# Blank records by scatter at steps 25 to 28 in place of eight clears at the start (chunk attention, then a cosine router)

## The chip, the cores and the metric

The kernel runs on one core of a Trainium2 chip. The metric is the device time of one execution in microseconds; the kernel before took 654.62 us in the median of three runs (653.24 to 658.43).

## The reference

Attention in chunks of 64, over 8 batches, 8 heads, 576 positions and 64 values per head; its output, 4608 tokens of 512 values, goes to a router that gives each token to one of 8 experts, a two-layer network with weights of its own.

```python
scores = scale * np.matmul(q_c, k_c.transpose(0, 1, 2, 4, 3))     # chunks of 64
attn = np.exp(scores - max); attn = attn / (sum + 1e-09)
x = (attn @ v_c)  ->  (4608, 512)

xn = x / (np.linalg.norm(x, axis=-1, keepdims=True) + 1e-06)
en = expert_emb / (np.linalg.norm(expert_emb, axis=-1, keepdims=True) + 1e-06)
logits = xn @ en.T / tau
expert_idx = np.argmax(logits, axis=1)
gate_w = softmax(logits)[np.arange(N), expert_idx]
for e in range(E):                      # E = 8, D = 512, F = 1024
    mask = expert_idx == e
    h = np.maximum(x[mask] @ w1[e], 0.0)
    out[mask] = gate_w[mask, None] * (h @ w2[e])
```

## The kernel before

All data are float32. The work has two stages.

**The attention stage** goes over 36 tiles of 128 tokens (NT = 36) in a software pipeline: a loop over steps t from -3 to 38, in which each step does a part of several tiles. For tile t + 7 it issues the loads of k and q (`load_qk`, L591; on the POOL queue from tile 4 on), for tile t + 5 those of v (`load_v`, L606; on the SP queue up to step 25, on POOL's from step 26). PE transposes k and q of tile t + 3 (L617), computes the scores of tile t + 2 (L633), transposes the weights of tile t (L659) and multiplies them with v (L672, `values`). DVE writes the result to `xr`, a ring of 8 slots of one tile each (L683), and POOL writes each token's number beside it (the iota at L689). PE transposes x of the tile before for the router (L701).

After every four tiles the router works on them as a batch: logits (L716), the choice of the expert (`pick`, L745 to L749), and two steps later `place`, which counts how many tokens of each expert came before and so gives each token its row (`dest`, L786). The counts are matmuls into `rt_ps`, a PSUM tile that the logits also use. From step 6 on `put` (L821) then sends one tile a step to DRAM: an indirect DMA on the POOL queue that writes each of the 128 records to its own row of `spots`. A record is 576 floats (2304 B): x, the logits, the square sum and the token's number. `spots` has R = 4864 rows for each expert, and behind them 64 spare rows from row SPARE on. A row number of SPARE or above is dropped by the scatter's bound. At step t it is tile t - 6 that is put, and step t + 2 reuses its slot in `xr`, so the scatter must have landed by then.

**The expert stage** works on blocks of two groups of 64 tokens, each group of one expert: it reads the rows of `spots` (`load_rows`, L153 and L159, on SP), computes the hidden layer and the result (L253, L342, L413), and scatters the rows to the output by token number (L432). The first four blocks (NE = 4) are fixed in advance as the first four groups of experts 0 and 7: rows 0 to 255 of each. Their loads are issued while the attention still runs: `load_early` at steps 26, 27, 28 and 33. They count on those rows being complete at step 25. For that, `count_early` at step 25 (L805 to L811) looks at how many tokens each expert has by then (the 20 tiles placed); where an expert has fewer than 256, it raises its count, so that later tokens go behind row 255. A place in the first 256 rows where no token came must hold a blank record: zeros, with a token number out of range.

Ahead of all that, `clear_first` writes such blank records to the first 256 rows of both experts and to the spare rows: nine DMAs of 64 records on the SP queue, two at each step from step 1 on. At the end of the attention stage `pad_places` does the same for the last, incomplete group of each expert, by four indirect DMAs with row numbers `pad_h`, most of which fall out of range.

The order of the instructions is the program's order on every engine; the queues of SP and POOL are worked through in order, and a DMA that must wait holds what stands behind it. On SP the first weights (w1 at step 28, w2 at step 30, 2 MB for each of two experts) stand behind the early loads. In `put`, a scatter is declared free of the early loads issued before it; an early load waits for all the scatters put before it.

Of the kernel before, what the change touches and what calls it, by code (L numbers as in the profile page):

```python
# [9 lines left out]
FP32 = mybir.dt.float32  # L10
BF16 = mybir.dt.bfloat16
I32 = mybir.dt.int32
AF = mybir.ActivationFunctionType
ALU = mybir.AluOpType
# [4 lines left out]
P = 128  # L19
# [6 lines left out]
def kernel(  # L26
# [11 lines left out]
    nc = tc.nc  # L38
    B, H, S, Dh = q.shape
    E, D = moe_expert_emb.shape  # L40
# [7 lines left out]
    G = P // 2  # L48
# [5 lines left out]
    NE = 4  # L54
# [23 lines left out]
    R = N + G * NE  # L78
    SPARE = E * R
# [38 lines left out]
    second = keep.tile([P, 1], FP32, name="second")  # L118
# [5 lines left out]
    def load_first(buf, rows):  # L124

        for s in range(2):
            e = (0, E - 1)[s]
            nc.sync.dma_start(out=whole(buf[s]), in_=rows[:, e : e + 1, :], max_dma_last_dim=4096)
# [41 lines left out]
    def first_rows(s, j, n):  # L170
        r0 = (0, E - 1)[s] * R + G * j
        return spots[r0 : r0 + G * n, :]
# [277 lines left out]
    with (  # L450
# [15 lines left out]
        blank = one.tile([P, W], FP32, name="blank")  # L466
# [18 lines left out]
        io = one.tile([P, NST], FP32, name="io")  # L485
# [10 lines left out]
        e_0 = one.tile([P, 1], FP32, name="e_0")  # L496
# [11 lines left out]
        full = one.tile([P, E], FP32, name="full")  # L508
# [2 lines left out]
        base_h = one.tile([P, E // 2], FP32, name="base_h")  # L511
        in_g = one.tile([P, 1], FP32, name="in_g")
        e_p = one.tile([P, 1], FP32, name="e_p")

        def constant_parts():
            nc.gpsimd.iota(io_i, pattern=[[1, NST]], base=0, channel_multiplier=0)
            nc.gpsimd.iota(part_i, pattern=[[0, 1]], base=0, channel_multiplier=1)
            nc.gpsimd.memset(blank, 0.0)
            nc.gpsimd.memset(blank[:, D + TOK : D + TOK + 1].bitcast(I32), NO_ROW)
            yield  # L520
            make_upper_triangular(nc, sltb, val=1.0, diag=False)
            nc.gpsimd.memset(onesb, 1.0)
            nc.gpsimd.tensor_copy(io, io_i)
            nc.gpsimd.tensor_copy(at, part_i)
            yield
            nc.gpsimd.tensor_scalar(pref, io[:, 0:E], -1.0, float(E), ALU.mult, ALU.add)
            nc.gpsimd.tensor_scalar(e_base, io[:, 0:E], float(R), None, ALU.mult)
            nc.gpsimd.memset(before, 0.0)
            nc.gpsimd.memset(eqb_all[:, 0], 0.0)
            nc.gpsimd.memset(ones, 1.0)  # L530
            yield
            nc.gpsimd.memset(jump[:, 1], 1.0)
            nc.gpsimd.memset(nb[:, 0:1], float((SPARE + R) // G))
            yield
            nc.gpsimd.tensor_scalar(second, at, float(G), None, ALU.is_ge)
            nc.gpsimd.tensor_scalar(is_0, at, 2.0, None, ALU.is_lt)
            yield
            nc.gpsimd.tensor_scalar(lim, at, -float(P), float(G * NE), ALU.mult, ALU.add)
            nc.gpsimd.tensor_scalar(step, second, -2.0, 1.0, ALU.mult, ALU.add)
            yield  # L540
            nc.gpsimd.tensor_scalar(first_s, second, -1.0, 1.0, ALU.mult, ALU.add)
            nc.gpsimd.tensor_scalar(back, io, -1.0, float(NST - 1), ALU.mult, ALU.add)
            yield
            nc.gpsimd.tensor_scalar(more_g, back, float(LEAST - NE), None, ALU.is_ge)
            nc.gpsimd.tensor_scalar(pair_g, back, float(LEAST - NE), None, ALU.is_equal)
            yield
            nc.gpsimd.tensor_tensor(more_g, more_g, pair_g, ALU.add)
            nc.gpsimd.tensor_tensor(pair_g, back, more_g, ALU.subtract)
            yield
            nc.gpsimd.memset(more_e[:, NSW - 1 : NSW], 1)  # L550
            nc.gpsimd.tensor_scalar(e_0, second, float(E - 1), None, ALU.mult)
            yield
            nc.gpsimd.tensor_scalar(e_1, e_0, 1.0, None, ALU.add)
            nc.gpsimd.tensor_scalar(ends_e, io[:, 0:E], 0.0, None, ALU.is_equal)
            yield
            nc.gpsimd.tensor_scalar(full, io[:, 0:E], float(E - 1), None, ALU.is_equal)
            nc.gpsimd.tensor_tensor(ends_e, ends_e, full, ALU.add)
            yield
            nc.gpsimd.tensor_scalar(done, ends_e, float(NE), None, ALU.mult)
            nc.gpsimd.tensor_scalar(ends_e, ends_e, is_0, None, ALU.mult)  # L560
            yield
            nc.gpsimd.tensor_scalar(in_g, second, -float(G), at, ALU.mult, ALU.add)
            nc.gpsimd.tensor_scalar(e_p, second, float(R), None, ALU.mult)
            yield
            nc.gpsimd.tensor_scalar(
                base_h, io[:, 0 : E // 2], 2.0 * R, e_p, ALU.mult, ALU.add
            )

        def clear_first():

            for j in range(NE):
                for s in range(2):
                    nc.sync.dma_start(out=first_rows(s, j, 1), in_=blank[0:G])
                    yield
            nc.sync.dma_start(out=spots[SPARE : SPARE + G, :], in_=blank[0:G])

        before = one.tile([P, E], BF16, name="before")
        qk_t, qkT, st = {}, {}, {}
# [221 lines left out]
        to_put = []  # L800

        def count_early():

            cnt = rt_ps[:, 3, 0]
            nc.tensor.matmul(cnt, lhsT=onesb, rhs=before, start=True, stop=True)  # L805

            nc.vector.tensor_scalar(full, cnt, -1.0, lim, ALU.mult, ALU.add)
            nc.vector.tensor_scalar(full, full, 0.0, float(P), ALU.max, ALU.min)
            with nc.allow_low_precision("whole numbers up to 36 + 128"):
                nc.vector.tensor_tensor(eqb_all[:, 0], full, ends_e, ALU.mult)  # L810
                nc.vector.tensor_tensor(before, before, eqb_all[:, 0], ALU.add)  # L811
# [6 lines left out]
        def put(n):  # L818

            for at, m in to_put[:n]:  # L820
                ins = nc.gpsimd.indirect_dma_start(  # L821
                    out=spots,
                    out_offset=bass.IndirectOffsetOnAxis(ap=at, axis=0),
                    in_=m,
                    in_offset=None,
                    bounds_check=SPARE - 1,
                    oob_is_err=False,
                )
                tc.declare_no_dep(ins.ins, group="spots", reason="each token has its own place")
                tc.add_to_no_dep_group("spots", ins.ins)  # L830
                for e in early_ins:
                    tc.declare_no_dep(
                        ins.ins, e.ins, reason="no place of these groups"
                    )
            del to_put[:n]
# [207 lines left out]
        early_t = 26  # L1043
# [6 lines left out]
        for t in range(-3, NT + 3):  # L1050

            if 0 <= t < NT:
                turn_a(t)
            if t == early_t - 1:
                count_early()

            for w in ahead_v[t]:
                load_v(w, nc.sync if t < early_t else nc.gpsimd)
            if t + 3 < NT:
                turn_qk(t + 3)  # L1060
                if t + 7 < NT:
                    load_qk(t + 7)
            if t - 2 in ends:
                logits(ends[t - 2])
            if t == NT:
                turn_x(t - 1)
            early_parts(t, 0)
            if 0 <= t + 2 < NT:
                scores(t + 2)
            if t - 2 in ends:  # L1070
                copy_logits(ends[t - 2])
            if 0 <= t - 1 < NT - 1:
                turn_x(t - 1)
            if t - 3 in ends:
                place(ends[t - 3])
            if 0 <= t < NT:
                values(t)
            if t == NT - 8:
                load_first(w1_sb, w1_rows)
            if t == NT - 6:  # L1080
                load_first([w[0] for w in w2_sb], w2_rows)
            if 0 <= t + 2 < NT:
                weights(t + 2)
            if t - 2 in ends:
                pick(ends[t - 2])
            if early_t <= t < early_t + XBUF:
                load_early(t - early_t)

            put(1 if t < NT - 2 else 2)
            if t == NT - 3:  # L1090
                turn_xb(0)
                load_early(XBUF)
            if t == NT - 1:
                turn_xb(1)
            early_parts(t, 1)
            if t == -2:
                turn_experts()
            if t >= 0:
                next(constants, None)
            if t >= 1:  # L1100
                next(clears, None)
                next(clears, None)
# [151 lines left out]
```

## Time and profile before

| What | Value |
|---|---|
| median of three runs | 654.62 us (653.24 to 658.43) |
| the profiled execution | 659.4 us, its span 657.6 us |
| PE busy | 620.0 us, 94% of the span |
| DVE, ACT, POOL busy | 427.6, 430.4, 183.8 us |
| attention stage | to about 180 us |
| DMA | 112.68 MB, 171 GB/s in the mean |
| clears of `spots` on SP | 20.4 to 33.6 us |
| step 25 to step 28, on PE | about 114 to 133 us |

The span is what the profile's times count from; the profiled execution's own time is a little longer than it. A line of a timeline gives the start in us, the duration in us, the engine, the line of the kernel, the operation with output and input, and the count; in brackets stands the idle time of the engine before it and what ended it. "SPq" is the SP queue, whose instructions issue DMAs. A line by stretches gives, for each engine, the busy time and the number of instructions.

### The profile page before, as it was taken

The page shows a single profiled execution, that of the slowest core. Times are in us where ns is not written, and L with a number is a line of the kernel's source. Part 1 is how long each engine was busy: PE and PEld are TensorE (multiplying, and loading weights), DVE is VectorE, ACT ScalarE, POOL GpSimd, SP SyncE. Part 2 cuts the span into 40 slices and gives each one's busy share as a digit, 9 for nine tenths or more (in the row PEclk, how much of TensorE's full clock was granted, in tenths as well). Part 3 has the DMA queues.
Part 4 walks back from the last instruction along what each step waited for, and adds up shares of the span by engine and source line. Part 5 has one row for each costly group of instructions (what it writes and reads, how often), then busy time and mean ns, then how long its engine had stood idle before and what let it go on. Part 6 is the DMA issues. An engine that isn't in the chain of part 4 may idle for free. (4 is left out here: it accounts for less than half of the span.)

```text
span 657.6 us, 24868 instructions
## 1 busy us (share of the span) xinstructions
PE 620.0 (94%) x9744; PEld 351.0 (53%) x9744; DVE 427.6 (65%) x1140; ACT 430.4 (65%) x758; POOL 183.8 (28%) x262
## 2 busy tenths in 40 slices
PE   6999998988799999999999999999999999999994
PEld 5777777865444445545555666444444444444441
DVE  4887888876479645656795466979645667565430
ACT  5766766755124767677767776777777677767650
POOL 7668887843221001002020102213001021000101
PEclk9999999989999999999999999999999999999998
DMA  9999898898518711111878111785921115411101
GB/s 252 321 276 268 260 280 265 260 340 323 214 38 303 299 44 55 39 46 38 304 262 321 59 41 45 288 308 197 350 78 59 42 44 176 165 42 35 50 27 42
DMA packets 91696, 112.68 MB, mean 171 GB/s; under 512 B 49260, under 2 KB 69484, under 8 KB 91560
## 3 DMA queue, kind: packets, MB, share of 16 engines
q1 hardware_dynamic: 79512, 71.99, 33.7%
q0 software_dynamic: 12016, 38.89, 17.2%
q8 instruction: 81, 1.33, 0.8%
q14 instruction: 55, 0.45, 0.2%
q10 hardware_dynamic: 32, 0.02, 0.0%
HBM read 334.71 MB, written 22.69 MB: 543 GB/s over the span
## 5 line engine op out<-in xcount | busy, mean ns | idle before, releaser
L413 PE MATMUL y_ps<-w,hT 128*32 128x512 f32 (+1 forms) x2368 | 280.6, 586 | 0.6 <-DMA w<-in_moe_w_dram 0.2
L361 ACT ACTIVATE h<-C 64x256 f32<-64x256 f32 x264 | 179.1, 679 | 72.8 <-DVE C L374 70.0
L413 PEld LDWEIGHTS y_ps<-w,hT 128*32 128x32 f32 x2368 | 94.9, 110 | 151.9 <-issue 132.9
L432 POOL DMA_INDIRECT out_dram<-y,spot x36 | 37.4, 1039 | 389.8 <-ACT y L425 314.3
L342 PE MATMUL h<-w,S 128*32 128x256 f32 x1056 | 106.5, 379 | 0.8 <-DVE w L291 0.8
L342 PE MATMUL h<-sums,xbT 128*32 128x256 f32 x1056 | 106.4, 379 | 0.6 <-DVEq L299 0.6
L374 DVE TENSOR_TENSOR C<-C,h 128x256 f32<-128x256 f32 x231 | 96.0, 416 | 11.6 <-PE h L342 4.4
L368 DVE STREAM_TRANSPOSE hT<-h 128x512 f32<-128x512 f32 x66 | 46.7, 708 | 54.8 <-ACT h L361 54.0
L342 PE MATMUL h<-w,xbT 128*32 128x256 f32 x1056 | 82.0, 379 | 0.0
L342 PEld LDWEIGHTS h<-w,S 128*32 128x32 f32 x1056 | 50.2, 110 | 22.6 <-DVE w L291 1.3
L342 PEld LDWEIGHTS h<-sums,xbT 128*32 128x32 f32 x1056 | 49.8, 110 | 22.7 <-DVEq L299 1.9
L342 PEld LDWEIGHTS h<-w,xbT 128*32 128x32 f32 x1056 | 44.4, 110 | 30.7 <-issue 8.4
L227 DVE TENSOR_SCALAR rn<-rn 128x1 f32<-128x1 f32 x37 | 5.6, 150 | 81.1 <-ACT rn L224 81.1
L425 ACT ACTIVATE y<-y_ps,gate 128x512 f32<-128x512 f32 x36 | 24.8, 688 | 43.7 <-issue 36.2
L342 PE MATMUL h<-sums,S 128*32 128x256 f32 x528 | 53.1, 379 | 0.0
L203 DVE STREAM_TRANSPOSE xbT<-xin 128x256 f32<-128x256 f32 x73 | 46.5, 675 | 0.5 <-DVE hT L368 0.5
L821 POOL DMA_INDIRECT spots<-xr,dest x36 | 37.4, 1039 | 29.0 <-DVE dest L786 9.9
L224 ACT ACT_TABLE_LOAD x34 | 43.6, 1283 | 0.9 <-issue 0.4
L231 ACT ACT_TABLE_LOAD x34 | 43.6, 1283 | 0.6
L703 ACT COPY xT<-tr 128x512 f32<-128x512 f32 x36 | 21.1, 586 | 33.7 <-PE tr L701 27.6
L591 POOL DMA_DIRECT2D kx<-in_k_dram x36 | 32.0, 890 | 12.2 <-PE tr L617 10.9
L591 POOL DMA_DIRECT2D qx<-in_q_dram x40 | 34.3, 861 | 0.7 <-PE tr L617 0.6
(204 smaller groups left out, 808.3 us busy)
## 6 DMA issues: line engine op xcount, KB each, us to landing
w<-in_moe_w_dram SPq DMA_DIRECT2D x74, 2048.0 KB
next_w<-in_moe_w_dram SPq DMA_DIRECT2D x67, 2048.0 KB
xin<-spots SPq DMA_DIRECT2D x158, 64.0 KB
qx<-in_q_dram POOLq DMA_DIRECT2D x32, 256.0 KB
v<-in_v_dram SPq DMA_DIRECT2D x58, 128.0 KB
kx<-in_k_dram POOLq DMA_DIRECT2D x28, 256.0 KB
spots<-blank SPq DMA_DIRECT2D x9, 144.0 KB
spot<-spots SPq DMA_DIRECT2D x80, 4.0 KB
```

The source lines that it names most:

```text
L203: nc.vector.transpose(xT[:, :, cols].rearrange("p c (b i) -> p b c i", i=Q), t[:, s * (D // 2) : (s + 1) * (D // 2)].rearrange("p (b i c) ...
L224: nc.scalar.activation(rn, spot[:, j % SPOTS, SQ : SQ + 1], AF.Sqrt)
L231: nc.scalar.activation(sh, sh, AF.Exp, accum_out=gate)
L342: nc.tensor.matmul(ps[t0 : t0 + Q], lhsT=a[:, c, s], rhs=w[:, r], start=c == 0, stop=c == KD // 2 - 1,)
L361: nc.scalar.activation(h[b][G * v : G * v + G, s].rearrange("p (k i) -> p k i", i=Q), x[G * s : G * s + G].rearrange("p (i k) -> p k i", i=Q),
L368: nc.vector.transpose(hT.rearrange("p k (s b i) -> p b s k i", b=2, i=Q)[:, b], h[b].rearrange("p s (k i) -> p s k i", i=Q),)
L374: nc.vector.tensor_tensor(out, a, b, op)
L413: nc.tensor.matmul(ps[Q * r : Q * r + Q, 0:w], lhsT=d["hT"][:, c, Q * t0 : Q * t0 + Q], rhs=w2_sb[s][buf_of(j)][:, c, d0 : d0 + w], start= ...
L425: nc.scalar.activation(y[:, 0:w], ps[:, 0:w], AF.Copy, scale=gate_of.pop(j))
L432: ins = nc.gpsimd.indirect_dma_start(out=to, out_offset=bass.IndirectOffsetOnAxis(ap=at, axis=0), in_=y[:, 0:w], in_offset=None, bounds_ch ...
L591: eng.dma_start(out=x[done : done + n], in_=src[b, :, s : s + n, :].rearrange("h p d -> p h d"),)
L821: ins = nc.gpsimd.indirect_dma_start(out=spots, out_offset=bass.IndirectOffsetOnAxis(ap=at, axis=0), in_=m, in_offset=None, bounds_check=S ...
```

## The change

The eight clears of the first rows go; the clear of the spare rows stays. In their place `count_early` works out, for every place of the first four groups, whether a token has come: `place_f` is the place's number in its expert's rows, `cnt_f` the expert's count, and `row_f` the row in `spots`; where the place is under the count, SPARE is added, so that the row is dropped. That gives 128 row numbers for each of the four groups of the pair of experts (`pad_f`), and at steps 25 to 28, after the tile's own scatter, one scatter of `blank` is put by them. Three operations for the constants are added on POOL at steps 15 and 16.

```diff
+        e_r = one.tile([P, 1], FP32, name="e_r")
+        cnt_f = one.tile([P, 1], FP32, name="cnt_f")
+        place_f = one.tile([P, NE], FP32, name="place_f")
+        row_f = one.tile([P, NE], FP32, name="row_f")
+        pad_f = one.tile([P, NE], I32, name="pad_f")
...
+            yield
+
+            nc.gpsimd.tensor_scalar(place_f, io[:, 0:NE], float(G), in_g, ALU.mult, ALU.add)
+            nc.gpsimd.tensor_scalar(e_r, e_0, float(R), None, ALU.mult)
+            yield
+            nc.gpsimd.tensor_scalar(row_f, place_f, e_r, None, ALU.add)
 
         def clear_first():
 
-            for j in range(NE):
-                for s in range(2):
-                    nc.sync.dma_start(out=first_rows(s, j, 1), in_=blank[0:G])
-                    yield
             nc.sync.dma_start(out=spots[SPARE : SPARE + G, :], in_=blank[0:G])
+            yield
...
             nc.tensor.matmul(cnt, lhsT=onesb, rhs=before, start=True, stop=True)
 
+
+            nc.vector.tensor_copy(full, cnt)
+            nc.vector.tensor_tensor(cnt_f, full[:, E - 1 : E], full[:, 0:1], ALU.subtract)
+            nc.vector.scalar_tensor_tensor(
+                out=cnt_f, in0=cnt_f, scalar=second, in1=full[:, 0:1], op0=ALU.mult, op1=ALU.add
+            )
+            nc.vector.tensor_scalar(place_f, place_f, cnt_f, float(SPARE), ALU.is_lt, ALU.mult)
+            nc.vector.tensor_tensor(pad_f, place_f, row_f, ALU.add)
             nc.vector.tensor_scalar(full, cnt, -1.0, lim, ALU.mult, ALU.add)
...
             put(1 if t < NT - 2 else 2)
+            if early_t - 1 <= t < early_t - 1 + NE:
+                j = t - (early_t - 1)
+                to_put.insert(0, (pad_f[:, j : j + 1], blank))
+                put(1)
```

## The prediction

> **What bounds the kernel now.** I read the page first (engine shares, slices), then busy time by stretch, the stages in which the edit lies, and there the timelines of PE, POOL, SP and DVE with the idle before each instruction.
>
> The page and the stretches (columns: stretch, its length, busy us and count of PE, PEld, DVE, ACT, POOL, granted clock, DMA share, GB/s):
>
> ```profile
> PE 620.0 (94%) x9744; PEld 351.0 (53%) x9744; DVE 427.6 (65%) x1140; ACT 430.4 (65%) x758; POOL 183.8 (28%) x262
> ...
> 20.00:40.00 20.00, 18.59 (x447) 15.94 (x450) 15.44 (x36) 13.60 (x32) 12.14 (x33) 1.00 1.08 317
> 60.00:80.00 20.00, 18.75 (x444) 15.64 (x446) 16.77 (x42) 14.02 (x31) 17.64 (x32) 1.00 0.88 257
> 140.00:160.00 20.00, 15.31 (x323) 11.77 (x318) 13.35 (x36) 10.27 (x24) 6.01 (x11) 0.91 0.91 347
> 240.00:260.00 20.00, 20.00 (x260) 8.91 (x254) 9.51 (x27) 13.94 (x23) 1.03 (x2) 1.00 0.14 39
> ```
>
> PE is the bound: 20.0 of 20 us in the expert stage (from about 180 us) and 18.6 to 18.8 in the attention stage. So a gain or loss counts only as PE idle time before 180 us; later nothing catches it up. The hole in PE is 140 to 160 us, after the four steps that get the new scatters.
>
> Where the clears stand, the PE timeline at the values (L672) of tiles 4, 8, 12, 16:
>
> ```profile
> 30.57 1.05 PE L672 MATMUL pv<-v,aT 64*64 64x65 f32 x32
> 47.05 0.70 PE L672 MATMUL pv<-v,aT 64*64 64x65 f32 x32
> 63.44 1.10 PE L672 MATMUL pv<-v,aT 64*64 64x65 f32 x32
> 79.89 0.70 PE L672 MATMUL pv<-v,aT 64*64 64x65 f32 x32
> ```
>
> Four tiles take 16.48, 16.39 and 16.45 us. The first four follow directly on the clears, whose issues end at 33.6 us, with the DMA share at 1.08 of 1; the others run long after. They differ by 0.1 us: the full DMA doesn't reach PE.
>
> The stretch of the new scatters, POOL's timeline, then SP's:
>
> ```profile
> 118.76 1.05 POOL L821 DMA_INDIRECT spots<-xr,dest  x1 [0.37 <-DMA v<-in_v_dram]
> 124.19 1.05 POOL L821 DMA_INDIRECT spots<-xr,dest  x1 [0.94 <-DVE rs L681]
> 128.85 1.05 POOL L821 DMA_INDIRECT spots<-xr,dest  x1 [0.18 <-POOL xr L689]
> 133.52 1.05 POOL L821 DMA_INDIRECT spots<-xr,dest  x1 [0.18 <-POOL xr L689]
> 135.75 1.05 POOL L821 DMA_INDIRECT spots<-xr,dest  x1 [0.35 <-POOL xr L689]
> 141.96 0.13 POOL L689 IOTA xr<- 128x1 int32 x1 [5.15 <-DMA spots<-xr,dest]
> 184.14 0.98 POOL L821 DMA_INDIRECT spots<-blank,pad_h  x1 [0.30 <-issue]
> ```
>
> ```profile
> 123.17 1.27 SPq L153 DMA_DIRECT2D xin<-spots  x2
> 128.35 1.12 SPq L153 DMA_DIRECT2D xin<-spots  x2
> 132.89 1.13 SPq L128 DMA_DIRECT2D w<-in_moe_w_dram  x2
> 134.86 8.35 SPq L153 DMA_DIRECT2D xin<-spots  x2
> ```
>
> The scatters of steps 25 to 29 (tiles 19 to 23) stand on a POOL with almost no slack: 0.37, 0.94, 0.18, 0.18, 0.35 us. At steps 26 to 28 POOL also issues the v loads (1.5 us a step), so a step costs it 4.66 us (124.19 to 128.85, 128.85 to 133.52).
>
> DVE and PE:
>
> ```profile
> 115.14 0.22 DVE L807 TENSOR_SCALAR full<-rt_ps,lim 128x8 f32<-128x8 f32 x1
> 141.99 0.69 DVE L683 TENSOR_TENSOR xr<-pv,rs 128x512 f32<-128x512 f32 x1 [1.60 <-DMA spots<-xr,dest]
> ```
>
> ```profile
> 115.41 1.08 PE L716 MATMUL rt_ps<-xT,enT 128*32 128x128 f32 x32 [0.64 <-DVE full L807]
> 142.82 0.63 PE L701 MATMUL tr<-ident,xr 128*128 128x128 f32 x4 [2.67 <-DVE xr L683]
> ```
>
> This decides: `xr` has 8 slots, so tile 30 can be written only when tile 22's scatter (133.52) has landed. It lands at about 141.9, 8.4 us after its start, because 4 MB of w1 were put in flight at 132.89. DVE waits 1.60 us for it and PE 2.67. A later scatter of tile 22 moves PE directly.
>
> **What the Trainium skill says.** "DMA: Bandwidth & Descriptors", section "Queues, rings and completion order": each DMA engine goes round between the queue rows with work, a packet at a time, and takes a ring's descriptors in order. The trace agrees in kind: a scatter lands in 4.4 us (118.76 to SP's wake at 123.17) without the weight load and in 8.4 us beside it. The same page, "Anatomy of one DMA — SWDGE (gpsimd) path", puts about 2.0 us fixed on such a DMA; here the last blank scatter, mostly dropped rows, starts at 184.14 and SP, which waits for it, goes on at 186.78: 2.6 us. "VectorE: DVE Perf Modes", section on the TRN2 errata, says that a small operation pays a fixed latency per instruction; here dependent ones of 128x8 start 0.20 to 0.28 us apart.
>
> **The change part by part.**
> *Removed:* eight clears of 64 x 2304 B, 1.18 MB, at 20.4 to 31.5 us on SP: eight issues of about 0.6 us, 4.9 us of a queue that otherwise waits for PE to free v slots. At 317 GB/s the bytes are 3.7 us of DMA. By the 16.48 against 16.39 us above I take 0.1 us gained; bounds 0 and 3.7.
> *POOL constants:* three operations of about 0.25 us at steps 15 and 16, where POOL still has waits: 0.
> *DVE at step 25:* five operations ahead of L807, four depending each on the one before. At 0.22 us, 1.1 us. PE's logits matmul (L716) already waits 0.64 us for L807 (they share `rt_ps`), so that wait grows by 1.1; PE has no other idle there. Bounds 0.3 and 1.3. It is part of the slip below, not added to it.
> *Four scatters:* 0.98 us by the pad_h row, 1.05 by the neighbours, and a gap of 0.2 to 0.3: 1.25 us each, on POOL behind the token's scatter of the step. From the reference's inputs the 20 tiles counted give experts 0 and 7 384 and 320 tokens, over the 256 cleared places, so all 512 rows fall out of range and no byte is written; only the instruction and its completion cost. That a dropped row is cheap in a DMA I take from the 2.6 us.
>
> POOL's schedule, in the times of before: scatter 19 at 118.76, pad to 121.05. Tile 20's waits for `dest` and DVE, 1.1 later: 125.3 (POOL is ready at 124.7). Then 4.66 + 1.25 a step: tile 21's 131.2, tile 22's 137.1, and tile 23's at 137.1 + 2.23 + 1.25 = 140.6. Slips: 1.1, 2.4, 3.6, 4.9.
>
> SP: the early loads of rows wait for all scatters put before, blank ones too. The first goes from 123.17 to about 123.8, the second from 128.35 to about 130 (blank at 126.4, behind the token's rows until 129.5); w1 stands behind it on SP, so 132.89 becomes about 134.5. Behind w1: the third rows, w2 and the fourth rows. w1 is used at 156.7 and w2 at 180.6; before, w2 waited for w1 and went at 152.8, so w1 has some 4 us to spare. Nothing there is late.
>
> Tile 22's scatter at 137.1 now starts 2.6 us after w1 instead of 0.6. With 8.4 us it lands at 145.5, a slip of 3.6; tile 23's, which before started 2.9 us after w1, took 9.6 (135.75 to 145.4), so 9 is as fair: 146.1, a slip of 4.2. Tile 23's lands at about 140.6 + 9.3 = 149.9 against 145.4: 4.5. From there the chain feeds itself: tile 24's scatter follows tile 30's iota, and tile 32 waits for it (before by 0.21 us on DVE). I see no slack up to the last `dest` that takes it back. Slip on PE 4.5 us, less 0.1: +4.4. Bounds: +1.1 (scatter delay absorbed, DVE alone) and +8 (w1 holds tile 22's rows longer, and PE's clock falls further after the longer stall; PE's transposes took 1.06 instead of 0.60 us just after 142.8).
>
> Sum against the profiled execution: 659.4 us (span 657.6 and 1.8 around it) + 4.4 = 663.8. It ran 4.8 us above the median of the runs; the difference is carried to the median: 654.6 + 4.4 = 659.0.
>
> **Rivals.** A measurement tells about 1% (6.5 us) from no change.
> 1. *POOL's slip, as worked out:* 659.0, its own range 656.5 to 662.5. Chance 0.48.
> 2. *Absorbed.* Because SP starts w1 later, tile 22's rows might get ahead of most of its packets and land in 4 to 5 us (137.1 + 5 = 142.1, as before). Then only DVE's 1.1 us is left, partly in the stall: 655.5. For it: 4.4 us without weights. Against it: the scatter is later than w1's issue. Chance 0.22.
> 3. *Other side: the clears held the first loads.* DMA at 1.08 in 20 to 40 us; kx and qx of tiles 5 to 8 queue beside 1.18 MB. Up to 3.7 us come back if those loads land after PE wants them, and it outweighs the loss only if the scatter slip also is under 2 us: 654.6 - 3.7 + 1.1 = 652.0. Against it: the equal four-tile times, and a single 1.17 us wait for v, at 20.55, for loads issued before the clears. Chance 0.15.
> 4. *A new chain of waits:* w1 outlasts tiles 22 to 25, each pair of scatters adds 2 to 3 us more, and the clock sags: 4.4 + 5 = 664. Chance 0.15.
>
> **The numbers.** The likeliest gives 659.0. The range runs from rival 3's 652.0 to a little over rival 4, 665.0. Over 661.2: a fifth of case 1 and most of case 4, 0.23. Under 648.1: a piece of case 3, 0.04. Within: 0.73.
>
> **What would show it.** Right: tiles 4 to 16 at 16.4 us per four; PE's wait for `full` at 1.5 to 1.8 us instead of 0.64; tile 22's scatter 3 to 4 us later; w1's issue 1 to 2 us later; the stall before tile 30 some 3 us longer; the same PE time from 190 us to the end. Wrong: an unmoved IOTA wait end at 142 (rival 2), four-tile times under 16 us before 64 us (rival 3), or stalls that grow again at tiles 32 to 34 (rival 4). A blank scatter taking much more than 1 us on POOL, or 4 us to land, breaks the price that all this rests on.

## The result and the profile after

The changed kernel takes 661.41 us in the median (659.09 to 663.74, 17 runs), the kernel before in the same runs 657.61 (652.17 to 661.67, 17 runs). The ratio is 1.0059, with a 95% interval of 1.004 to 1.0078: some 3.9 us slower, 0.6%. The forecast was +4.4 us, with a chance of 0.73 that the change stays within 1%; the median of 654.6 from which it started was that of three runs.

The pair of profiles doesn't show this. The profiled execution after took 659.09 us, the fastest of its 17 runs, and its span is 657.3 us against 657.6. So the profiles have to be read stage by stage. First the page's shares and the stretches after, with the same columns as before:

```profile
PE 618.9 (94%) x9744; PEld 344.2 (52%) x9744; DVE 426.6 (65%) x1145; ACT 428.9 (65%) x758; POOL 189.2 (29%) x269
...
20.00:40.00 20.00, 19.78 (x475) 16.93 (x475) 16.40 (x37) 14.61 (x34) 13.10 (x34) 1.00 0.98 271
60.00:80.00 20.00, 19.20 (x491) 16.40 (x493) 17.23 (x42) 14.91 (x34) 17.77 (x31) 1.00 1.00 275
140.00:160.00 20.00, 16.49 (x346) 12.78 (x349) 13.18 (x34) 10.27 (x23) 6.44 (x11) 0.83 0.93 351
```

PE is busier in 20 to 40 us (19.78 against 18.59), where the clears are gone, but also in 60 to 80 us, far from them. The clock in 140 to 160 us is lower, 0.83 against 0.91. PE's timeline at the values of tiles 4, 8, 12 and 16:

```profile
30.39 1.05 PE L680 MATMUL pv<-v,aT 64*64 64x65 f32 x32
46.06 0.69 PE L680 MATMUL pv<-v,aT 64*64 64x65 f32 x32
61.35 0.69 PE L680 MATMUL pv<-v,aT 64*64 64x65 f32 x32
76.60 0.69 PE L680 MATMUL pv<-v,aT 64*64 64x65 f32 x32
```

Four tiles take 15.67, 15.29 and 15.25 us, not the 16.4 that was forecast. The kernel reaches the count of step 25 3.7 us sooner than before. How much of that belongs to the change is what the experiments have to tell.

The stretch of the new scatters, POOL's and SP's timelines after:

```profile
114.40 1.05 POOL L837 DMA_INDIRECT spots<-xr,dest  x1 [0.18 <-POOL xr L697]
115.75 1.01 POOL L837 DMA_INDIRECT spots<-blank,pad_f  x1 [0.30 <-DMA v<-in_v_dram]
120.54 1.05 POOL L837 DMA_INDIRECT spots<-xr,dest  x1 [0.26 <-POOL xr L697]
126.60 1.05 POOL L837 DMA_INDIRECT spots<-xr,dest  x1 [0.18 <-POOL xr L697]
132.68 1.05 POOL L837 DMA_INDIRECT spots<-xr,dest  x1 [0.18 <-POOL xr L697]
136.06 1.02 POOL L837 DMA_INDIRECT spots<-xr,dest  x1 [0.17 <-POOL xr L697]
141.38 0.13 POOL L697 IOTA xr<- 128x1 int32 x1 [4.30 <-DMA spots<-xr,dest]
```

```profile
127.59 1.14 SPq L153 DMA_DIRECT2D xin<-spots  x2
131.15 1.13 SPq L128 DMA_DIRECT2D w<-in_moe_w_dram  x2
```

And the operations of DVE and PE that wait:

```profile
111.41 0.22 DVE L823 TENSOR_SCALAR full<-rt_ps,lim 128x8 f32<-128x8 f32 x1
141.41 0.69 DVE L691 TENSOR_TENSOR xr<-pv,rs 128x512 f32<-128x512 f32 x1 [5.21 <-DMA spots<-xr,dest]
```

```profile
111.69 1.08 PE L724 MATMUL rt_ps<-xT,enT 128*32 128x128 f32 x32 [1.10 <-DVE full L823]
142.25 1.09 PE L709 MATMUL tr<-ident,xr 128*128 128x128 f32 x4 [6.31 <-DVE xr L691]
```

A blank scatter takes 1.01 us and a gap of 0.30 on POOL. Four of them that wrote all their rows would add 1.18 MB to the queue that takes POOL's transfers. Its line of the page, first before, then after, has the same 38.89 MB, so the rows are dropped:

```profile
q0 software_dynamic: 12016, 38.89, 17.2%
```

```profile
q0 software_dynamic: 12336, 38.89, 17.5%
```

POOL's steps are 6.06 and 6.08 us long (120.54, 126.60, 132.68) where they were 4.66, and DVE waits 5.21 us for tile 22's scatter where it waited 1.60. Counted from the count's operation (L823 at 111.41, before L807 at 115.14), the scatters of tiles 20 to 23 come at 9.1, 15.2, 21.3 and 24.7 us against 9.1, 13.7, 18.4 and 20.6, and w1 at 19.7 against 17.8. Tile 30 is written at 30.0 against 26.9: 3.1 us later. The five new operations that stand ahead of the count's come on top: 1.05 us from their first start, at 110.36, to L823.

One more thing appears that the profile of before did not show. PE stands in the result of the fifth block:

```profile
236.13 9.18 PE L413 MATMUL y_ps<-w,hT 128*32 128x512 f32 x62 [3.96 <-DMA w<-in_moe_w_dram]
```

Before, it was:

```profile
238.92 6.63 PE L413 MATMUL y_ps<-w,hT 128*32 128x512 f32 x58 [0.24 <-DMA w<-in_moe_w_dram]
```

From the fourth block's output to the fifth's it is 19.6 us after and 14.0 before; an undisturbed block takes 12.9.

### The profile page after: what moved, and what is told of

Same layout as the page of the kernel before. It is cut to its first block, busy times and chain, and to the rows that moved or that the text cites. A ratio compares the mean times of both kernels' runs of the same rounds, so it can differ in the third digit from the quotient of the medians.

```text
span 657.3 us, 24875 instructions
## 1 busy us (share of the span) xinstructions
PE 618.9 (94%) x9744; PEld 344.2 (52%) x9744; DVE 426.6 (65%) x1145; ACT 428.9 (65%) x758; POOL 189.2 (29%) x269
## 3 DMA queue, kind: packets, MB, share of 16 engines
q0 software_dynamic: 12336, 38.89, 17.5%
## 5 line engine op out<-in xcount | busy, mean ns | idle before, releaser
L413 PEld LDWEIGHTS y_ps<-w,hT 128*32 128x32 f32 x2368 | 90.6, 110 | 157.9 <-issue 136.4
L342 PEld LDWEIGHTS h<-w,S 128*32 128x32 f32 x1056 | 48.7, 110 | 24.3 <-DVE w L291 1.5
L342 PEld LDWEIGHTS h<-w,xbT 128*32 128x32 f32 x1056 | 43.0, 110 | 32.3 <-issue 9.0
L203 DVE STREAM_TRANSPOSE xbT<-xin 128x256 f32<-128x256 f32 x73 | 44.2, 643 | 0.5 <-DVE hT L368 0.5
L709 PE MATMUL tr<-ident,xr 128*128 128x128 f32 x144 | 23.3, 286 | 12.5 <-DVE xr L691 10.5
```

The source lines that it names most:

```text
L203: nc.vector.transpose(xT[:, :, cols].rearrange("p c (b i) -> p b c i", i=Q), t[:, s * (D // 2) : (s + 1) * (D // 2)].rearrange("p (b i c) ...
L342: nc.tensor.matmul(ps[t0 : t0 + Q], lhsT=a[:, c, s], rhs=w[:, r], start=c == 0, stop=c == KD // 2 - 1,)
L413: nc.tensor.matmul(ps[Q * r : Q * r + Q, 0:w], lhsT=d["hT"][:, c, Q * t0 : Q * t0 + Q], rhs=w2_sb[s][buf_of(j)][:, c, d0 : d0 + w], start= ...
```

## The experiments

They ran in three sets of four, each set beside the kernel before on one chip. The medians of before were 657.09, 663.85 and 656.70 us, so kernels are compared by their ratios, and closely only within a set. The runs are called e1 to e12, in the order in which they stand here. "Measured" is the ratio to before, with its 95% interval.

**First set: the parts (e1 to e4).** e1 is the kernel with the clears gone and nothing in their place; of the change only the three constants on POOL stay. Against the changed kernel:

```diff
-            nc.vector.tensor_copy(full, cnt)
...
-            nc.vector.tensor_tensor(pad_f, place_f, row_f, ALU.add)
...
-                to_put.insert(0, (pad_f[:, j : j + 1], blank))
-                put(1)
```

> Leaves out the blank records of the first groups altogether (no clears, no row numbers, no blank scatters); with these inputs every one of those rows gets a token. Theory (POOL's slip is the loss, the clears are hidden): ratio 0.998 to 1.001, PE's time at tile 25's step within 1 us of before's typical. Rival (the clears hold the first loads): ratio 0.994 or less, and four tiles in about 15.3 to 15.7 us between tiles 4 and 16, as in the one profile of the changed kernel, where before's has 16.4. If so, the changed kernel's scatters cost more than the 0.6% that is seen.

Measured: 0.9963 (0.9941 to 0.9984), 655.16 us. The clears did cost, about 0.37% or 2.4 us (1.1 to 3.9), though less than the 0.6% at which the rival began. The 16.4 us did not hold as a mark: with the clears, tiles 8 to 12 took 15.45 and 15.56 us in the profiles of the next two kernels.

e2 has the clears and the scatters together (the change, with the eight clears put back):

```diff
         def clear_first():
 
+            for j in range(NE):
+                for s in range(2):
+                    nc.sync.dma_start(out=first_rows(s, j, 1), in_=blank[0:G])
+                    yield
```

> Both: the eight clears stay and the four blank scatters with their row numbers are added. Theory: the loss is all from what is added, ratio 1.005 to 1.008, tile 22's scatter lands some 4 us later relative to step 25, PE waits 5 to 6 us before tile 30. Rival (clears cost something too): 1.008 to 1.013, clearly above the changed kernel.

Measured: 1.0085 (1.0058 to 1.0113), 662.92 us: what is added costs 5.6 us (3.8 to 7.4). Tile 30 is written 30.0 us after the count's operation, as in the changed kernel.

e3 has the row numbers alone, with the clears and without the scatters (the same, with `to_put.insert` and its `put` left out):

> Clears stay; the five DVE operations at step 25 and the three constants on POOL are added, no blank scatter. Theory: PE's wait for the count at step 25 grows by 1.1 us, most of it taken up in the stall before tile 30: ratio 1.000 to 1.002. Rival (the DVE operations are the loss): 1.004 or more.

Measured: 1.0028 (1.0007 to 1.0048), between the two expectations. About 1.8 us of the loss (0.5 to 3.2) are the numbers', the three constants on POOL with them. That leaves 0.57%, 3.7 us, for the scatters. DVE's wait in this kernel's timeline is the short one again:

```profile
138.42 0.69 DVE L695 TENSOR_TENSOR xr<-pv,rs 128x512 f32<-128x512 f32 x1 [2.14 <-DMA spots<-xr,dest]
```

That is 26.5 us after its count's operation (111.88): the 3.5 us up to 30.0 come with the scatters.

e4 is the changed kernel again:

> The changed kernel once more, for a second profile and to be compared with its parts in the same runs. Theory: ratio 1.004 to 1.008; the stall before tile 30 on DVE is 4 to 6 us again, while the time at which step 25 is reached differs from the first profile by some us, since it differs from run to run. Rival (the early lead of 4.8 us at step 25 in the first profile belongs to the change): step 25's count at 110 to 111 us again, against 115 for kernels with clears.

Measured: 1.0047 (1.0027 to 1.0067). The parts add up: -0.37 + 0.85 = +0.48%. The count's operation came at 113.3 us, not at 111.4; with the clears it came at 111.9 (e3), 113.8 (e2) and 115.1 (before). So most of the 3.7 us of lead in the first pair of profiles was chance. DVE waits 5.53 us before tile 30, again 30.0 us after the count.

**Second set: POOL's queue, SP's order, the clears doubled (e5 to e8).** In e5 the v loads of steps 26 to 28 go from POOL to SP:

```diff
-                load_v(w, nc.sync if t < early_t else nc.gpsimd)
+                load_v(w, nc.sync if t < early_t + 3 else nc.gpsimd)
```

> The changed kernel with the v loads of steps 26 to 28 issued on SP, ahead of each step's early load, instead of POOL. That takes 4.6 us of issues off POOL in the very steps of the blank scatters and leaves their number and order as they are. Theory (the loss is POOL's queue running late): tile 22's scatter starts before or with w1, the wait of DVE before tile 30 falls from 5.2 to 5.5 us to under 2, and the ratio to before falls from 1.005 to 0.997 to 1.001. Rival (the blank scatters cost as DMAs, by holding the early loads on SP): the wait before tile 30 stays above 4 us, ratio 1.003 to 1.007.

Measured: 0.9987 (0.9959 to 1.0015): no loss is seen against before, though the same blank scatters are put in the same places. DVE has no wait before tile 30:

```profile
144.13 0.69 DVE L691 TENSOR_TENSOR xr<-pv,rs 128x512 f32<-128x512 f32 x1
```

POOL's steps are 4.57 us now, and tile 22's scatter starts at 134.35, 0.9 us before w1 (135.23) instead of 1.5 us after it. A smaller wait, 0.97 us, is found at tile 32. The edit moves two things, POOL's queue and SP's: tile 22's scatter starts 19.8 us after the count (21.3 in the changed kernel), and w1 20.6 us after it (19.7).

In the next run but one, e7, the attention stage is that of the changed kernel, on the same chip, and there DVE waits:

```profile
147.00 0.69 DVE L691 TENSOR_TENSOR xr<-pv,rs 128x512 f32<-128x512 f32 x1 [5.01 <-DMA spots<-xr,dest]
```

That is 33.7 us after its count's operation; e5 has 29.5. Beside the changed kernel's profiles from outside this set (30.0 to 30.5 us) e5 gains little, and there is one profile of each, so the comparison is good only within the set.

e6, the kernel before with the same move:

> The kernel before with the same move of the v loads. Theory: the stall of 1.6 to 2.1 us on DVE before tile 30 goes too, as tile 22's scatter starts some 4 us sooner, ahead of w1: ratio 0.993 to 0.998. Rival (w1's traffic decides, not POOL's queue): 0.999 to 1.002, the wait merely found at another tile.

Measured: 0.9982 (0.9961 to 1.0003), at the line between the two. The stall before tile 30 is gone here too, but a wait of 0.96 us stands two tiles later, and the end hardly moves. Something else had to hold the end.

e7, another order on SP in the expert stage:

> The changed kernel, with one order on SP altered in the expert stage: the second layer's weights of block 4 are asked for ahead of the rows of block 8. In every profile but that of before, PE stands 4 us in block 4's result for an issue that SP reaches some 51 to 53 us after the last blank scatter of the attention stage. Theory now: the end is set by SP's chain of loads from that last scatter on, so whatever delays the attention's tail is carried by SP and not by PE; with the order altered PE's stall of 4 us and the slower clock after it go, ratio to before 0.992 to 0.998. Rival (PE's own lateness carries the loss, as the prediction had it): the stall is waiting that PE would do anyway, ratio 1.003 to 1.007 as for the changed kernel.

```diff
-                    if n + XBUF < NJ:
+                    if n + XBUF < NJ and j != NE - 1:
                         load_x(n + XBUF)
...
                 load_w2(next_of(j))
+            if j == NE - 1:
+                load_x(n + XBUF)
```

Measured: 1.0046 (1.0019 to 1.0074). Taken alone this speaks for the rival, but the changed kernel did not run in this set, in which before was 7 us slower than in the others, and the profile had the block's stall gone. The third set has both kernels.

e8, each clear of the kernel before done twice:

> The kernel before with each of the eight clears followed by another of the same size to rows of experts 3 and 4 that are written over later: the removed cost doubled. Theory from the first runs (the clears cost 0.2 to 0.6% by filling the DMA just as PE wants its next instructions and rows): ratio 1.003 to 1.008, and PE's gap in the middle of tile 5's values (0.5 to 2.2 us with the clears, 0 or 1.4 without) at 1 us or more. Rival (no such cost; the difference without the clears is chance): 0.999 to 1.001.

```diff
                     nc.sync.dma_start(out=first_rows(s, j, 1), in_=blank[0:G])
+                    r0 = (3, 4)[s] * R + G * j
+                    nc.sync.dma_start(out=spots[r0 : r0 + G, :], in_=blank[0:G])
                     yield
```

Measured: 1.0073 (1.0039 to 1.0106), so clears do cost. But the gap in tile 5's values was not there. The timelines of POOL and of DVE show another way:

```profile
46.78 1.11 POOL L823 DMA_INDIRECT spots<-xr,dest  x1 [7.60 <-DMA v<-in_v_dram]
...
50.61 0.69 DVE L685 TENSOR_TENSOR xr<-pv,rs 128x512 f32<-128x512 f32 x1 [4.41 <-DMA spots<-xr,dest]
56.26 0.69 DVE L685 TENSOR_TENSOR xr<-pv,rs 128x512 f32<-128x512 f32 x1 [2.56 <-DMA spots<-xr,dest]
```

The first scatter stands 7.6 us on POOL for a DMA, 2.7 to 5 us later than the 41.8 to 44.1 us in the profiles of before, of the changed kernel and of the first set. The issues of the doubled clears run up to 41 us here, and the scatter must follow all of them; the trace names a v load, so that this was the wait is likely and not shown. `xr`'s ring runs full behind it. With eight clears this wait isn't seen: the first scatter waits 1.4 to 1.8 us in all five profiles with them, for ACT or DVE. So doubling shows that clears cost, and not how eight do.

**Third set: the end of the chain (e9 to e12).** e9 is the changed kernel once more:

> The changed kernel as it is, so that the next three can be read beside it on one chip. Expected ratio 1.004 to 1.008, as in both sets of runs so far.

Measured: 1.0087 (1.0055 to 1.0118).

e10 has e7's order:

> The changed kernel with block 4's second weights asked for ahead of block 8's rows, again, now beside the changed kernel: the first run gave 1.0046 on another chip, where the changed kernel itself was not run, and its profile showed the 4 us stall in block 4's result gone. Theory (SP's chain carries the end): 0.3% or more under the changed kernel in the same runs. Rival (no effect; PE carries it): within 0.2% of it.

Measured: 0.9962 (0.9942 to 0.9982), 1.2% under the changed kernel in the same set, and under before. On SP the request for w2 now follows the weights of the first layer at once. First the changed kernel's line, then e10's:

```profile
236.02 1.76 SPq L177 DMA_DIRECT2D w<-in_moe_w_dram  x2
```

```profile
230.62 1.34 SPq L177 DMA_DIRECT2D w<-in_moe_w_dram  x2
```

In the changed kernel PE goes on at 236.13, 0.1 us after SP reaches the request, and from 236 to 240 us the DMA moves 4 GB/s. So PE waits for SP to come to this load, which carries a condition (`cond` in `load_when`), and not for weights to arrive. The outputs of the fourth and fifth block, in POOL's timeline, first of the changed kernel:

```profile
227.18 0.98 POOL L432 DMA_INDIRECT out_dram<-y,spot  x1 [11.08 <-DMA xin<-spots]
246.80 0.98 POOL L432 DMA_INDIRECT out_dram<-y,spot  x1 [18.64 <-ACT y L425]
```

and of this kernel:

```profile
227.65 0.98 POOL L432 DMA_INDIRECT out_dram<-y,spot  x1 [11.07 <-DMA xin<-spots]
240.56 0.98 POOL L432 DMA_INDIRECT out_dram<-y,spot  x1 [11.93 <-ACT y L425]
```

19.6 us become 12.9, from nothing but an order on SP, though both attention stages end within half a microsecond of each other (last blank scatter at 181.88 and 182.36). PE had been early and waited for SP. In the ten profiles without this order (the changed kernel's and before's among them), PE's wait for w2 ends 54.3 to 55.6 us after the start of the attention stage's last blank scatter (before: 184.14 to 238.92; after: 181.88 to 236.13). In between SP issues the row loads and the weights in order. (The 51 to 53 us in the expectation of e7 count from SP's first load behind that scatter.)

How long PE waits there differs: 2.2 to 4.6 us in six of the ten, but only 0.20 to 0.24 in before's profile and in e5, e6 and e8, which are all of the second set that have the first order. On that chip PE was hardly early, so e7 had little to remove. That would fit its 1.0046; with one profile of each kernel it isn't shown.

e11 is the kernel before with both moves, the v loads on SP and w2 first:

> The kernel before with both moves: v loads of steps 26 to 28 on SP and block 4's second weights ahead of block 8's rows. If both waits were on the path: 0.990 to 0.997. If only the v loads count: 0.997 to 0.999, as alone (0.998).

Measured: 0.9894 (0.9851 to 0.9936), 650.28 us (six runs), the lowest ratio here: the clears stay, and it is faster than before and than the changed kernel. Tile 22's scatter starts 15.4 us after the count (18.4 before), and tile 30 isn't held:

```profile
127.71 1.05 POOL L821 DMA_INDIRECT spots<-xr,dest  x1 [0.18 <-POOL xr L689]
...
137.34 0.69 DVE L683 TENSOR_TENSOR xr<-pv,rs 128x512 f32<-128x512 f32 x1
```

e12, the changed kernel with both moves:

> The changed kernel with both moves. The clears gone are worth 0.37% by the first set, the DVE numbers cost 0.28%, and the blank scatters little once POOL has room: so about equal to the kernel before with both moves, 0.990 to 0.998. If the blank scatters still cost through the early loads that wait for them on SP, it is 0.3% or more above that one.

Measured: 0.9942 (0.992 to 0.9964), 0.5% above e11, with intervals that overlap. With both moves in both kernels the change still looks like a loss, and by more than the 0.3% that the expectation names as the sign that the blank scatters also cost through the early loads on SP. POOL's steps are 4.6 us with the blank scatters and 3.2 without. On SP the early loads do wait for blank scatters, 4.2 us in two waits, yet w1 isn't later than in e11 but sooner, 19.6 us after the count against 24.5. So tile 23's scatter starts 2.1 us behind w1 (in e11 3.7 ahead of it), and tile 31, which takes its slot, is held:

```profile
143.25 0.69 DVE L691 TENSOR_TENSOR xr<-pv,rs 128x512 f32<-128x512 f32 x1 [2.52 <-DMA spots<-xr,dest]
```

How much of the 0.5% belongs to POOL and how much to SP's order isn't separated.

## Why the prediction was right, and where its steps were not

The direction and the size held: +4.4 us forecast, +3.9 measured. That is partly two errors of the sum that cancelled.

- *POOL's queue* was right. The slips were forecast as 1.1, 2.4, 3.6 and 4.9 us; with the 1.05 us of the numbers they are 1.1, 2.5, 3.9 and 5.1. A blank scatter costs POOL 1.3 us (forecast 1.25) though its rows are all dropped. The scatters cost 3.7 us (e2 against e3), and with them tile 30 comes 3.5 us later. That the cost comes by POOL being late behind w1 is borne out by e5, where POOL has room: 0.9987, against 1.0046 in e7, whose attention stage is the changed kernel's; their intervals don't overlap. It isn't proved, for e5 also moves w1 back on SP. And e5 has the gain from the clears: beside e6 (0.9982) what is added may still cost some 0.4%, if the clears are worth 0.37% on that chip too. That the early loads, held by the blank scatters, cost something of their own is not ruled out (e12).
- *Tile 22's scatter behind w1* was right: landing 3.1 us later from the count and 4.2 with the numbers, forecast 3.6 to 4.2. DVE's wait grew by 3.6, forecast "some 3". Rival 2 is out: tile 22's scatter landed 8.7 us after its start, not 4 to 5. So is rival 4: DVE waits for no scatter at tiles 31 to 34.
- *The clears* were the term most mis-sized: "I take 0.1 us gained", measured 2.4 (1.1 to 3.9), inside the stated bounds of 0 to 3.7. The step that failed is the reading of equal four-tile times in one profile, in which the attention stage was slow all along (16.4 us also at tile 16). A cost in the first four tiles could not be told from that. The sign named for rival 3, four tiles in under 16 us, did appear in the changed kernel (15.67, 15.29, 15.25), but kernels with the clears show it too (e2, e3). The way in which eight clears cost is open. The four tiles from 4 to 8 took 16.1 to 18.5 us in the five profiles with eight clears (mean 16.9) and 15.2 to 16.8 in the eight without (mean 15.9), which is 1 us of the 2.4; part of it is gaps in PE that the trace puts down to no engine, such as 2.22 us in the middle of tile 5's values in e2, but e4, without the clears, has 1.40 there.
- *The DVE operations* were put inside the slip at 1.1 us. Their length is right (1.05), but PE's wait for the count grew only from 0.64 to 1.10 us, not to 1.5. With the constants they cost 1.8 us (0.5 to 3.2); why it should be more than their length isn't settled, and the interval allows that it is less.
- *"Later nothing catches it up"* was wrong about who carries the loss. PE isn't full from 180 us on: in before's profile it is busy for 19.58 us of 180 to 200 and 19.16 of 200 to 220. In the changed kernel's three profiles it is early and waits 4 us for SP in the fifth block, and loses 2 to 3 more to the slower matmuls behind the stall. That SP's order held the end there is shown by e10 beside e9, and only on that chip; e7 on another was no faster than before. The delay reaches SP through the last blank scatter, from which SP's chain starts: within the first set that comes 67.4 and 67.0 us after the count's operation in e1 and e3, without the new scatters, and 71.4 and 70.6 in e2 and e4, with them. Profiles from elsewhere lie less far apart (before 69.0, after 70.5).
- *The sum*: -2.4 for the clears against -0.1, and +5.6 for what is added against +4.5; the parts give +3.2 (each holds the three constants on POOL, so these count twice), the direct comparisons +3.1 to +5.7.

## What to carry to other kernels

Here an indirect DMA that writes nothing costs its queue as much as one that writes (1.01 against 1.05 us); before one is added, look at the queue's slack in that very stretch and at which buffer comes free late behind it. When the bound engine is busy all through the last stage, check that nothing it needs has an issue order of its own: an SP queue that asks for things in the wrong order can hold the end back though the engine shows 94%. And one profile of each kernel can mislead by more than the effect; the same mark should be read in several before a term is put at nothing.

## What was not expected of the hardware

- Matmuls after a stall were slow: behind 3.96 us of waiting, 62 result matmuls took 9.18 us, and without the stall (e10) 62 took 7.04. The granted clock was 0.57 from 236 to 240 us, behind the stall, and 1.00 from 240 to 246; in e10 it was 1.00 from 230 to 240. In the five profiles that waited 4.0 to 4.6 us there, the 62 took 8.73 to 9.90 us.
- The same kernel's attention stage differs by some us between executions: the changed kernel reached the count's operation at 111.4, 113.3 and 111.9 us in three profiles.
